# State update ahead of the state read, and the first chunk reordered with M first, long lines and whole weight pieces

## The chip, the cores and the metric

The kernel runs on one core of one Trainium2 chip. Times are device microseconds (us) of one execution. Before: median 628.86 us of the four runs taken beside the changed kernel (626.38 to 630.35). The granted clock of TensorE is given where it matters.

PE is TensorE, PEld its weight load, DVE is VectorE, ACT is ScalarE, POOL is GpSimd, SP is SyncE; SPq and ACTq are the queues in which SP and ACT issue transfers. L311 is line 311 of the kernel concerned.

## The reference

An mLSTM cell (4 batches, 8 heads, 768 steps, head size 40) is followed by a two-layer block with exact GELU (320 to 2048 to 320). The weights of the block come as 64-bit floats.

```python
for t in range(S):
    m_new = np.maximum(f_gate[:, :, t] + m, i_gate[:, :, t])
    C = exp(f + m - m_new) * C + exp(i - m_new) * (v outer k)     # n likewise, with k
    y[:, :, t] = sigmoid(o_gate) * (C q) / max(|n q|, 1)
...
x = attn_out.transpose(0, 2, 1, 3).reshape(B * S, H * D)
h = x @ w_in
g = 0.5 * h * (1.0 + erf(h / sqrt(2)))
return g @ w_out
```

## The kernel before

The 768 steps are cut into 6 chunks of 128. For each chunk and batch the cell computes scores (k times q), multiplies them with weights W made from the running maximum M, reads the state with q, updates the state with k and v, and turns the result y into xT. "Up" (xT times w_in, then GELU) and "down" (g times w_out) follow for all four batches at once. Down matmuls of one chunk fill the gaps of the cell of the next. During the first chunk, the weights are loaded as raw 64-bit words and converted to 32-bit floats in 26 pieces: 10 of w_in, 16 of w_out.

The parts that matter here, cut:

```python
# weight pieces: two transfers of 64 partitions each, lines of 1 KB
src = w_src["in"][blk * R:(blk + 1) * R, 2 * f0:2 * (f0 + 2 * WP)]
src = src.rearrange("k (m two x) -> k m two x", two=2, x=2 * P)
pieces.append(([(slice(R * e, R * e + R), src[:, :, e, :]) for e in range(2)], w_in[...]))
...
def fetch(i):
    bits[i] = raw.tile([P, WP, 2], U32, name="bits", tag="bits", bufs=NB)[...]
    for r, src in parts:
        nc.sync.dma_start(out=bits[i][r]..., in_=src)

def scores(self, b):
    ...                                          # ps: k times q; then W = ps * W on DVE
    pf = ps_h.tile([P, H + NP, D1], F32, name="pf", tag="h")
    pc = pf[:, H:H + NP, :]                      # read and update share one bank
    if c > 0:
        ...nc.tensor.matmul(pf[r, ...], qT[:, p, r], state[b][:, p, :])       # read
        nc.vector.tensor_tensor(out=self.far[b], in0=pf[:, 0:H, :], in1=gT)   # far
    if c + 1 < NCH:
        ...nc.tensor.matmul(pc[...], kb[n % NLD][...], vw[...])               # update
        ...                                      # state = state * dec + pc (POOL, DVE)

def values(self, b):                             # ph = W times v; hs = ph (+ far); y from hs

for n in range(B):                               # SP, at the start
    if n > 0:
        load(n)                                  # q, k, v, output gate of one batch
    fetch(n)
```

## Time and profile before

| | before |
|---|---|
| median of 4 runs | 628.86 us |
| span of the profiled execution | 627.3 us, granted clock 0.961 |
| first up matmul | 70.14 us |
| cell of chunk 1 resumes on PE | 127.90 us |
| up of chunks 1 to 5 starts at | 184.19, 278.68, 373.16, 467.63, 554.50 us |
| PE waits ahead of the update, chunks 1 to 4 | 19.5 us in 16 waits |
| DVE waits for pieces of w_in | 9.3 us in 4 waits |

The start times divide the kernel in two: up to about 128 us the converting of weights and the first cell set the pace, and after that every chunk takes 94.5 us with PE nearly full. Two lines of before that the prediction doesn't show are wanted later. The first is from the page's 40 slices (15.7 us each): the mean busy share of the core's 16 DMA engines, in tenths.

```profile
DMA  9999199735430034530034530035200010000000
```

In the first seven slices (110 us) the transfer engines are full, except in slice 5. The second is from DVE's waits (line waited for: us in total, times, longest):

```profile
DVE pow L219 <- DMA bits<-in_moe_w_in_dram: 9.3, 4, 3.3
```

`pow` is the first operation of a piece's conversion, `bits` the raw piece. The conversions seldom wait for their data.

### The profile page before, as it was taken

What the parts mean: (1) busy time and instruction counts of PE and PEld (TensorE: products, weight loads), DVE (VectorE), ACT (ScalarE), POOL (GpSimd) and SP (SyncE); (2) the same over time, 40 slices, a digit from 0 to 9 for tenths busy, and PEclk for the clock granted to TensorE, in tenths of its full rate; (3) what the DMA queues carried; (4) which work ended last, traced back from release to release, by engine and by line L of the source; (5) the groups of instructions that cost most, each with busy time, mean ns of one, the idle gap of its engine ahead of it and who ended that gap; (6) DMA issues with size and microseconds to landing.
All of it is one profiled execution on the core that took longest, in us unless ns stands there. A gap on an engine that the chain in (4) does not pass through costs nothing.

```text
span 627.3 us, 9450 instructions
## 1 busy us (share of the span) xinstructions
PE 554.4 (88%) x3850; PEld 358.1 (57%) x3850; DVE 199.0 (32%) x442; ACT 230.1 (37%) x516; POOL 81.3 (13%) x130
## 2 busy tenths in 40 slices
PE   0637698778999998899999899999899999999997
PEld 0536354456764466764476664476664477754575
DVE  5457686834630013630013630013630014500000
ACT  0775274683022283022284022284022293122200
POOL 4212300012230011230011230011220001100000
PEclk9967699889999999999999999999999999999999
DMA  9999199735430034530034530035200010000000
GB/s 161 208 211 184 37 161 207 178 104 103 76 64 0 1 112 90 82 64 2 0 108 92 81 67 1 0 101 96 46 22 0 1 44 13 11 11 0 1 21 21
DMA packets 136233, 43.62 MB, mean 70 GB/s; under 512 B 101248, under 2 KB 134048, under 8 KB 136192
## 3 DMA queue, kind: packets, MB, share of 16 engines
q1 hardware_dynamic: 132976, 41.36, 33.3%
q10 hardware_dynamic: 3216, 1.67, 1.0%
q8 instruction: 30, 0.49, 0.4%
q14 instruction: 11, 0.09, 0.1%
HBM read 38.99 MB, written 4.03 MB: 69 GB/s over the span
## 4 chain that ended last, share of the span: by engine, by line
PE 49%; issue 38%; POOL 6%; DMA 3%; SPq 2%; DVE 1%; POOLq 0%; ACTq 0%; ACT 0%; DVEq 0%
PE po L403 25%; PE pu L388 11%; PE ph L329 3%; PE ps L293 3%; POOL state L320 2%; POOL Mb L254 2%; DMA Mb<-M_d 2%; PE pf L303 2%; PE pf L311 2%; PE pt L276 2%; SPq L102 2%; PE px L355 1%; SPq L208 1%; POOL vw L286 1%; DMA M_d<-M 1%
## 5 line engine op out<-in xcount | busy, mean ns | idle before, releaser
L403 PE MATMUL po<-w_out,g 128*128 128x320 f32 x768 | 221.0, 437 | 0.0
L388 PE MATMUL pu<-xT,w_in 64*128 64x512 f32 x960 | 215.5, 604 | 3.2 <-ACT g L391 2.8
L403 PEld LDWEIGHTS po<-w_out,g 128*128 128x128 f32 x768 | 141.2, 191 | 52.6 <-issue 1.2
L388 PEld LDWEIGHTS pu<-xT,w_in 64*128 64x128 f32 x960 | 100.6, 192 | 115.7 <-issue 109.5
L296 DVE TENSOR_TENSOR W<-ps,W 128x512 f32<-128x512 f32 x48 | 30.9, 685 | 259.0 <-PE ps L293 259.0
L391 ACT ACTIVATE g<-pu 128x512 f32<-128x512 f32 x96 | 52.0, 593 | 131.9 <-PE pu L388 131.9
L357 ACT COPY xT<-px 64x384 f32<-64x384 f32 (+1 forms) x48 | 17.9, 420 | 128.3 <-DVE xT L356 128.3
L257 ACT ACTIVATE W<-Mb,aT 128x128 f32<-128x128 f32 x192 | 58.1, 393 | 1.8 <-POOL Mb L254 1.7
L320 POOL TENSOR_TENSOR state<-state,dec 64x164 f32<-64x164 f32 x32 | 14.8, 462 | 286.2 <-PE pf L303 285.0
L311 PE MATMUL pf<-vw,kb 128*64 128x41 f32 x320 | 14.1, 239 | 32.1 <-POOL state L320 19.5
L254 POOL TENSOR_SCALAR_AFFINE_SELECT Mb<-Mb 128x1024 f32<-128x1024 f32 x24 | 27.0, 1145 | 80.2 <-DMA Mb<-M_d 80.0
L406 ACT COPY o_sb<-po 128x320 f32<-128x320 f32 x24 | 10.2, 426 | 61.5 <-PE po L403 40.7
L311 PEld LDWEIGHTS pf<-vw,kb 128*64 128x64 f32 x320 | 12.2, 146 | 35.0 <-POOL state L320 21.7
L338 POOL TENSOR_TENSOR y<-hs,ob 128x320 f32<-128x320 f32 x24 | 19.4, 809 | 97.8 <-DVE hs L332 72.1
L293 PEld LDWEIGHTS ps<-qT,kT 64*128 64x128 f32 x384 | 25.8, 205 | 10.1 <-issue 10.1
L293 PE MATMUL ps<-qT,kT 64*128 64x128 f32 x384 | 30.4, 302 | 0.0
L329 PE MATMUL ph<-vb,W 128*64 128x41 f32 x768 | 28.6, 236 | 0.0
L329 PEld LDWEIGHTS ph<-vb,W 128*64 128x64 f32 x768 | 26.4, 145 | 2.4 <-issue 2.2
L356 DVE COPY xT<-px 64x384 f32<-64x384 f32 (+1 forms) x48 | 21.1, 476 | 17.5 <-PE px L355 16.7
L276 PE MATMUL pt<-ident,kb 128*128 128x128 f32 x96 | 17.2, 308 | 9.3 <-ACT kT L279 9.3
L279 ACT COPY kT<-pt 128x512 f32<-128x512 f32 x24 | 14.0, 584 | 30.8 <-PE pt L276 30.6
L355 PE MATMUL px<-ident,y 128*128 128x128 f32 x120 | 18.4, 287 | 6.8 <-ACT xT L357 6.0
(71 smaller groups left out, 352.9 us busy)
## 6 DMA issues: line engine op xcount, KB each, us to landing
Mb<-M_d SPq DMA_DIRECT2D x21, 512.0 KB, 4.0
bits<-in_moe_w_in_dram SPq DMA_DIRECT2D x20, 256.0 KB, 5.6
bits<-in_moe_w_out_dram SPq DMA_DIRECT2D x16, 320.0 KB, 4.2
qb<-in_q_dram SPq DMA_DIRECT2D x24, 160.0 KB, 4.4
kb<-in_k_dram SPq DMA_DIRECT2D x24, 160.0 KB, 4.8
vb<-in_v_dram SPq DMA_DIRECT2D x24, 160.0 KB, 4.3
ob<-in_o_gate_dram SPq DMA_DIRECT2D x24, 160.0 KB, 3.9
out_dram<-o_sb SPq DMA_DIRECT2D x24, 160.0 KB, 1.8
```

What stands on the lines that cost most here:

```text
L254: nc.gpsimd.affine_select(out=M_n, in_=M_n, compare_op=OP.is_ge, fill=1.0e30, base=0, pattern=[[0, H], [1, L]], channel_multiplier=-1)
L257: nc.scalar.activation(out=W[n][:, h, :], in_=M_n[:, h, :], func=AF.Exp, scale=-1.0, bias=aT[:, c, b * H + h:b * H + h + 1])
L276: nc.tensor.transpose(pt[:, p, :], src[n % NLD][:, 2 * p:2 * p + 2, :].rearrange("p h d -> p (h d)"), ident)
L293: nc.tensor.matmul(ps[hip][:, p, :], kT[r, p, :], qT[r, p, :], start=True, stop=True)
L296: nc.vector.tensor_tensor(out=w, in0=ps[hip], in1=w, op=OP.mult)
L311: nc.tensor.matmul(pc[halves[hip], p, :], kb[n % NLD][:, 2 * p + hip, :], vw[:, 2 * p + hip, :], start=True, stop=True)
L320: nc.gpsimd.tensor_tensor(out=st, in0=st, in1=d.to_broadcast([DP, NP, D1]), op=OP.mult)
L329: nc.tensor.matmul(ph[r, h, :], Pm[:, h, r], vb[n % NLD][:, h, :], start=True, stop=True)
L355: nc.tensor.transpose(px[:, k, :], ys[:, (k0 + k) * R:(k0 + k + 2) * R], ident)
L388: nc.tensor.matmul(pu[e], w_in[r, k, f // 2 * P:(f // 2 + 1) * P], xT[r, (k - e) % NK, :], start=(k == 0), stop=(k == NK - 1))
L391: nc.scalar.activation(out=g[:, f + e, :], in_=pu[e], func=AF.Gelu)
L403: nc.tensor.matmul(po, g[:, f, b * L:(b + 1) * L], w_out[:, f, :], start=(f == 0), stop=(f == NF - 1))
```

## The change

There are two intents. In the cell, the update goes ahead of the read in their common bank, so that PE doesn't wait for DVE's `far` between the two. In the first chunk, M of the chunk is computed alone and sent first, into four buffers instead of three and in long lines; the work of the batches is put in the order in which tiles should arrive; and each weight piece becomes one transfer with lines of 4 KB.

The diff, cut to its core:

```diff
@@ weight pieces
-            src = src.rearrange("k (m two x) -> k m two x", two=2, x=2 * P)
-            pieces.append(([(slice(R * e, R * e + R), src[:, :, e, :]) for e in range(2)],
-                           w_in[:, blk, f0 // 2:f0 // 2 + WP]))
+            pieces.append((src.rearrange("k (two x) -> two k x", two=2), w_in[:, blk, f0 // 2:f0 // 2 + WP]))
...
-        for r, src in parts:
-            to = bits[i][r].rearrange("p n two -> p (n two)")
-            if len(src.shape) == 3:
-                to = to.rearrange("p (m x) -> p m x", x=2 * P)
-            nc.sync.dma_start(out=to, in_=src)
+        nc.sync.dma_start(out=bits[i].rearrange("p n two -> p (n two)"), in_=src)
@@ M first
-    NM = 3
+    NM = 4
-    M_d = dram.tile([BH, S], F32, name="M_d")
+    M_d = dram.tile([NCH, BH, L], F32, name="M_d")
+    for c0, c1 in ((0, 1), (1, NCH)):            # scans of chunk 0 alone, then of the rest
...
+        if c0 == 0:
+            nc.scalar.dma_start(out=M_d[0], in_=M[:, 0])
+            for n in range(B):
                 load_M(n, nc.scalar)
@@ scores
             pc = pf[:, H:H + NP, :]
+            if c + 1 < NCH:
+                (the 8 update matmuls)
             if c > 0:
                 (the 8 read matmuls, far)
             if c + 1 < NCH:
-                (the 8 update matmuls)
                 (scaling and adding of the state)
@@ first chunk
+        def run_first(self):
+            self.turn(0), weights_of(0), convert(0)
+            decays()
+            self.scores(0), weights_of(1), convert(1)
+            self.turn(1), weights_of(2), weights_of(3), output_gate(0), self.values(0), convert(2)
+            self.scores(1), self.turn_y(0), output_gate(1), self.values(1), convert(3)
+            self.turn(2), self.scores(2), self.turn_y(1), output_gate(2), self.values(2), convert(4)
+            self.turn(3), self.scores(3), self.turn_y(2), output_gate(3), self.values(3), convert(5)
+            self.turn_y(3)
```

`turn` transposes k and q of a batch (kT, qT), `weights_of` makes W from M, `turn_y` transposes y into xT, `convert` handles one weight piece, and `decays` prepares the decay factors of the state. The up steps are renumbered for the columns that a piece now holds; their number and sizes stay.

More of the change, by code (lines that the diff above doesn't have):

```diff
@@ L53 @@
     NLD = 6
-    NM = 3
+    NM = 4
     NB = 4
     WP = 512
-    assert S % L == 0 and DFF % (4 * WP) == 0 and DM % R == 0 and DM <= WP and D <= DP and NLD > B == 4
+    assert S % L == 0 and DFF % (4 * WP) == 0 and DM % R == 0 and DM <= WP and D <= DP and NLD > B == NM == 4
     const = ctx.enter_context(tc.tile_pool(name="const", bufs=1))
@@ L112, in load_M @@
         Mb[n] = wts.tile([P, H, L], F32, name="Mb", tag="Mb", bufs=NM)
-        eng.dma_start(out=Mb[n], in_=M_d[b * H:(b + 1) * H, c * L:(c + 1) * L]
-                      .unsqueeze(0).to_broadcast([P, H, L]))
+        eng.dma_start(out=Mb[n].rearrange("p h l -> p (h l)"),
+                      in_=M_d[c, b * H:(b + 1) * H, :].rearrange("h l -> (h l)").unsqueeze(0).to_broadcast([P, H * L]))
     nc.sync.dma_start(out=f_sb.rearrange("p c l -> p (c l)"), in_=f_gate.rearrange("b h s -> (b h) s"))
@@ L146 @@
     nc.vector.memset(m0[:, 0:1], -1.0e30)
-    nc.vector.tensor_tensor_scan(out=bl.rearrange("p c l -> p (c l)"), data0=keep.rearrange("p c l -> p (c l)"),
-                                 data1=f_sb.rearrange("p c l -> p (c l)"), initial=0.0, op0=OP.mult, op1=OP.add)
-    nc.vector.tensor_tensor(out=a, in0=i_sb, in1=bl, op=OP.subtract)
-    for c in range(NCH):
-        nc.vector.tensor_tensor_scan(out=M[:, c], data0=a[:, c], data1=a[:, c], initial=m0[:, c:c + 1],
-                                     op0=OP.max, op1=OP.max)
-        if c == 0:
-            nc.scalar.dma_start(out=M_d[:, 0:L], in_=M[:, 0])
-            for n in range(NM):
+    for c0, c1 in ((0, 1), (1, NCH)):
+        flat = lambda t: t[:, c0:c1].rearrange("p c l -> p (c l)")
+        nc.vector.tensor_tensor_scan(out=flat(bl), data0=flat(keep), data1=flat(f_sb), initial=0.0,
+                                     op0=OP.mult, op1=OP.add)
+        nc.vector.tensor_tensor(out=a[:, c0:c1], in0=i_sb[:, c0:c1], in1=bl[:, c0:c1], op=OP.subtract)
+        for c in range(c0, c1):
+            nc.vector.tensor_tensor_scan(out=M[:, c], data0=a[:, c], data1=a[:, c], initial=m0[:, c:c + 1],
+                                         op0=OP.max, op1=OP.max)
+            if c + 1 < NCH:
+                nc.vector.tensor_tensor(out=m0[:, c + 1:c + 2], in0=bl[:, c, L - 1:L], in1=M[:, c, L - 1:L],
+                                        op=OP.add)
+        if c0 == 0:
+            nc.scalar.dma_start(out=M_d[0], in_=M[:, 0])
+            for n in range(B):
                 load_M(n, nc.scalar)
-        if c + 1 < NCH:
-            nc.vector.tensor_tensor(out=m0[:, c + 1:c + 2], in0=bl[:, c, L - 1:L], in1=M[:, c, L - 1:L], op=OP.add)
-    nc.scalar.dma_start(out=M_d[:, L:S], in_=M[:, 1:NCH].rearrange("p c l -> p (c l)"))
     nc.vector.tensor_tensor(out=ew, in0=a[:, 0:NCH - 1],
@@ L165, with gates_turned, decays @@
                             in1=M[:, 1:NCH], op=OP.subtract)
+    def gates_turned(parts):
+        for src, dst in parts:
+            n = dst.shape[1]
+            pg = ps_tr.tile([P, n, BH], F32, name="pg", tag="tr")
+            for c in range(n):
+                nc.tensor.transpose(pg[:, c, :], src[:, c, :], ident[0:BH, 0:BH])
+            nc.vector.tensor_copy(out=dst, in_=pg)
+    gates_turned([(a, aT)])
     nc.scalar.activation(out=ew, in_=ew, func=AF.Exp)
     nc.scalar.activation(out=gg, in_=gg, func=AF.Exp)
-    for src, dst in ((a, aT), (ew, ewT), (gg, gT)):
-        n = dst.shape[1]
-        pg = ps_tr.tile([P, n, BH], F32, name="pg", tag="tr")
-        for c in range(n):
-            nc.tensor.transpose(pg[:, c, :], src[:, c, :], ident[0:BH, 0:BH])
-        nc.vector.tensor_copy(out=dst, in_=pg)
-    pd = ps_tr.tile([P, NCH - 1, BH], F32, name="pd", tag="tr")
-    nc.tensor.matmul(pd.rearrange("p c n -> p (c n)"), last, gT.rearrange("p c n -> p (c n)"), start=True, stop=True)
-    nc.vector.tensor_copy(out=dec, in_=pd)
-    gate_ctx.close()
-    gp = ctx.enter_context(tc.tile_pool(name="gp", bufs=1))
+    def decays():
+        gates_turned([(ew, ewT), (gg, gT)])
+        pd = ps_tr.tile([P, NCH - 1, BH], F32, name="pd", tag="tr")
+        nc.tensor.matmul(pd.rearrange("p c n -> p (c n)"), last, gT.rearrange("p c n -> p (c n)"),
+                         start=True, stop=True)
+        nc.vector.tensor_copy(out=dec, in_=pd)
     w_src = {}
@@ L190 @@
             src = w_src["in"][blk * R:(blk + 1) * R, 2 * f0:2 * (f0 + 2 * WP)]
-            src = src.rearrange("k (m two x) -> k m two x", two=2, x=2 * P)
-            pieces.append(([(slice(R * e, R * e + R), src[:, :, e, :]) for e in range(2)],
-                           w_in[:, blk, f0 // 2:f0 // 2 + WP]))
+            pieces.append((src.rearrange("k (two x) -> two k x", two=2), w_in[:, blk, f0 // 2:f0 // 2 + WP]))
     n_in = len(pieces)
     for f in range(NF):
-        pieces.append(([(slice(0, P), w_src["out"][f * P:(f + 1) * P, :])], w_out[:, f, :]))
+        pieces.append((w_src["out"][f * P:(f + 1) * P, :], w_out[:, f, :]))
     bits, sig, pow2 = {}, {}, {}
@@ L201, in fetch @@
             return
-        parts, dst = pieces[i]
+        src, dst = pieces[i]
         bits[i] = raw.tile([P, WP, 2], U32, name="bits", tag="bits", bufs=NB)[:, 0:dst.shape[1], :]
-        for r, src in parts:
-            to = bits[i][r].rearrange("p n two -> p (n two)")
-            if len(src.shape) == 3:
-                to = to.rearrange("p (m x) -> p m x", x=2 * P)
-            nc.sync.dma_start(out=to, in_=src)
+        nc.sync.dma_start(out=bits[i].rearrange("p n two -> p (n two)"), in_=src)
     def convert(i):
@@ L235, in convert @@
             fetch(i + NB)
-    for n in range(B):
-        if n > 0:
-            load(n)
-        fetch(n)
+    fetch(0)
+    load(1)
+    fetch(1)
+    load(2)
+    fetch(2)
+    load(3)
+    fetch(3)
+    nc.sync.dma_start(out=M_d[1:NCH].rearrange("c p l -> p c l"), in_=M[:, 1:NCH])
     halves = (slice(0, R), slice(R, P))
@@ L299, in scores @@
             pc = pf[:, H:H + NP, :]
+            if c + 1 < NCH:
+                for p in range(NP):
+                    for hip in range(2):
+                        nc.tensor.matmul(pc[halves[hip], p, :], kb[n % NLD][:, 2 * p + hip, :], vw[:, 2 * p + hip, :],
+                                         start=True, stop=True)
             if c > 0:
@@ L308, in scores @@
             if c + 1 < NCH:
-                for p in range(NP):
-                    for hip in range(2):
-                        nc.tensor.matmul(pc[halves[hip], p, :], kb[n % NLD][:, 2 * p + hip, :], vw[:, 2 * p + hip, :],
-                                         start=True, stop=True)
                 for hip in range(2):
@@ L380, in up_steps, with step @@
     def up_steps(g):
-        def step(f):
+        def step(i):
+            f = i // (WP // P) * 2 * (WP // P) + i % (WP // P)
             pu = [ps_mm.tile([P, TG], F32, name="pu", tag="mm") for e in range(2)]
-            for k in range(NK):
+            for blk in range(NK):
                 for e in range(2):
                     r = halves[e]
-                    nc.tensor.matmul(pu[e], w_in[r, k, f // 2 * P:(f // 2 + 1) * P], xT[r, (k - e) % NK, :],
-                                     start=(k == 0), stop=(k == NK - 1))
+                    nc.tensor.matmul(pu[e], w_in[r, blk, i * P:(i + 1) * P], xT[r, (blk - e) % NK, :],
+                                     start=(blk == 0), stop=(blk == NK - 1))
             for e in range(2):
-                nc.scalar.activation(out=g[:, f + e, :], in_=pu[e], func=AF.Gelu)
-        return [lambda f=f: step(f) for f in range(0, NF, 2)]
+                nc.scalar.activation(out=g[:, f + e * (WP // P), :], in_=pu[e], func=AF.Gelu)
+        return [lambda i=i: step(i) for i in range(NF // 2)]
     def down_steps(c, g):
@@ L417, in feeder @@
         return fill
-    conv = feeder([lambda i=i: convert(i) for i in range(len(pieces) + 1)])
-    first = feeder([lambda: conv(1)] * (n_in // 2 + 1))
-    Cell(0).run(first)
+    Cell(0).run_first()
+    gate_ctx.close()
+    gp = ctx.enter_context(tc.tile_pool(name="gp", bufs=1))
+    conv = feeder([lambda i=i: convert(i) for i in range(n_in // 2 + 1, len(pieces) + 1)])
     for c in range(NCH):
```

## The prediction

> **What bounds the kernel now.** I read the page first: busy shares, then the 40 slices.
>
> ```profile
> span 627.3 us, 9450 instructions
> PE 554.4 (88%) x3850; PEld 358.1 (57%) x3850; DVE 199.0 (32%) x442; ACT 230.1 (37%) x516; POOL 81.3 (13%) x130
> ...
> PE   0637698778999998899999899999899999999997
> ```
>
> PE is busy for 88% of the span, and the holes sit in two places: slices 1 to 8 (the first chunk, with the weights being converted) and one thin slice per chunk after it. So the two halves of the change hit two different regimes, and I size each by its own stage. The table of stretches (cut at round numbers near the first and last up matmuls of the timeline; busy us with counts for PE, PEld, DVE, ACT, POOL, then granted clock, DMA share, GB/s) says the same:
>
> ```profile
> 45.00:70.00 25.00, 16.02 (x206) 13.74 (x202) 19.15 (x41) 11.91 (x27) 8.76 (x10) 0.70 0.74 136
> 70.00:105.00 35.00, 34.57 (x140) 17.71 (x140) 24.94 (x56) 20.29 (x35) 0.00 (x0) 0.91 0.85 157
> 128.00:184.00 56.00, 51.12 (x476) 38.93 (x476) 24.43 (x54) 21.27 (x56) 14.21 (x20) 0.97 0.47 94
> 184.00:219.00 35.00, 35.00 (x163) 15.68 (x163) 0.00 (x0) 9.48 (x17) 0.00 (x0) 1.00 0.02 5
> ```
>
> From 128 us on, PE has no company in being full: 51.1 of 56 us in a cell stretch, 35 of 35 in an up stretch, granted clock 0.97 to 1.00. The 4.9 us that are missing in the cell stretch are one gap, four times. The timeline of one batch shows it:
>
> ```profile
> 141.69 1.16 PE L293 MATMUL ps<-qT,kT 64*128 64x128 f32 x16
> 142.78 0.79 PE L303 MATMUL pf<-state,qT 128*64 128x82 f32 x16
> 142.95 1.29 DVE L296 TENSOR_TENSOR W<-ps,W 128x512 f32<-128x512 f32 x2 [5.79 <-PE ps L293]
> 143.66 1.00 POOL L320 TENSOR_TENSOR state<-state,dec 64x164 f32<-64x164 f32 x2 [5.80 <-PE pf L303]
> 144.16 0.49 DVE L306 TENSOR_TENSOR far<-pf,gT 128x328 f32<-128x328 f32 x1
> 144.79 0.67 PE L311 MATMUL pf<-vw,kb 128*64 128x41 f32 x16 [1.22 <-POOL state L320]
> 145.25 1.14 PE L329 MATMUL ph<-vb,W 128*64 128x41 f32 x32
> ```
>
> The label "POOL state" is misleading. In program order the scaling of the state comes after these matmuls, so they cannot depend on it. L311 waits on DVE and on POOL; its POOL input (vw) is long done. DVE's far (L306), which reads the other part of the same pf tile, ends at 144.65, and PE goes 0.14 later; L320 merely ends at the same moment. The view of waits has the sum: PE pf L311 <- POOL state, 19.5 us in 16 waits.
>
> In the first chunk the chain of waits goes through the fourth M tile:
>
> ```profile
> 34.18 0.53 SPq L113 DMA_DIRECT2D Mb<-M_d  x1
> 41.24 1.09 POOL L254 TENSOR_SCALAR_AFFINE_SELECT Mb<-Mb 128x1024 f32<-128x1024 f32 x1 [19.63 <-DMA Mb<-M_d]
> 42.30 0.74 POOL L286 TENSOR_TENSOR vw<-vb,ewT 128x328 f32<-128x328 f32 x1
> 43.10 1.08 PE L311 MATMUL pf<-vw,kb 128*64 128x41 f32 x16 [10.53 <-POOL vw L286]
> ```
>
> With three buffers the fourth M waits for a buffer and for its turn on SP, lands at 41.1, holds POOL, POOL holds vw, and PE stands for 10.5 us. The first up matmul starts at 70.14.
>
> **What the Trainium skill says.** "PSUM — Partial Sum Buffer", section "PSUM bank collisions raise a hardware error": PE and VectorE must not touch one bank and quadrant together, even at other columns, so the wait is guarded by bank. The trace agrees: L311 writes other columns than far reads, and still starts only after far. The order, not the wait, has to change. "DMA: Bandwidth & Descriptors", "Rules for kernel authors", advises one 128-partition transfer instead of two to disjoint halves, which is what the weight pieces become. The trace of before has only the halves (median landing 5.8 us under load); it cannot yet say. "TensorE: Matmul & The Clock Gate", Part 1, gives half clock after an idle window and full clock after about 3.4 us of sustained work. The trace has a mean granted clock of 0.63 at 43 to 56 us and 0.60 at 70 to 78, and the up matmuls stay slow for about 6 us, longer than the page says.
>
> **Part 1: update ahead of read, chunks 1 to 4.** Nothing is added or removed: 8 update and 8 read matmuls per batch exchange places. The update needs vw, which POOL finished well before (147.86 + 0.74 = 148.60 for the batch whose scores start at 153.85), and the bank, which was free for the read anyway. The read then follows with no reader in between, and values (L329) use another bank. So each of 4 x 4 batches loses the 1.22 us gap: 16 x 1.22 = 19.5 us. A check: a cell stretch of chunk 4 from its end of up to the next up is about 59.9 us (94.5 us period less 34.6); that of the last chunk, which has no update, is 554.57 - 502.24 = 52.3. The difference 7.6 is 4 x (1.22 + 0.67), gap plus update, exactly. Does a new wait replace it? DVE now gets far 0.67 us later, at scores + 2.55 instead of + 2.47, because its two products W (1.29 us) end only there; the POOL scaling ends at about + 3.5, DVE's addition at about + 4.3, hs at about + 4.8, against 146.43 + 0.50 - 141.69 = + 5.2 before. y is needed two down parts later. The last turn of y in a chunk (y ready at 178.25, used at 181.40) has 3 us of slack. I find nothing, so all 19.5 us count, since PE is full up to the end.
>
> **Part 2: the first chunk.** What arrives sooner: the scan over chunk 0 alone takes 0.5 us in place of 1.75, the subtraction 0.25 in place of 0.94, so M_d is issued at about 4.4 instead of 6.3, and lands near 9. Four M loads follow by 12; at 512 KB and the 300 GB/s of the stretch after 13 us they take 1.4 to 1.7 us each, so the last is there by 17 to 20 instead of 41. The 10.5 us wait at 43 goes. But the new order is serial: turn(b) stands behind values(b-1) and a conversion. By hand, with the durations of before: ACT free at 12; table 1.28, two exponentials 1.45, kT and qT 1.1, W of batch 0 2.45: 17.8; conversion (two of 0.72) and state 2.0; W 2.45, conversion 1.45, kT and qT 1.1, two W 4.9, table 1.28, sigmoid 0.39, hs 0.43: hs of batch 0 ends near 32 (before: 49.99). Batch 1 to hs: den and y on DVE 2.1, five conversion operations 2.95, W 1.29, values 1.5, copy 0.5: 8.3, so 40.5. Batches 2 and 3 each go den 2.1, first conversion operation 0.45, two on ACT 1.45, kT and qT 1.1, scores 1.7, update 0.75, turn of y 1.3, values 1.5, hs 0.5: 10.9 with PE at its low clock, 9.5 with the full one. That gives hs of batch 3 at 62 (59.5), where before it was 64.3. Tail: den 2.1, conversion 3, copy of xT 0.5 to 0.9: up begins at 68 (65.5) instead of 70.14. The 18 us head start is nearly eaten by 11 us per batch, where before took 5.9, 4.7 and 3.7. Gain: 2 to 5 us, I take 2.5.
>
> **After it**, up and conversion of chunk 0 run from 70.14 to the end of PE's wait at 127.9 (6.97 us for ACT kT). That stretch is paced by 20 conversions (DVE 2.1 us each for the output weights, DMA share 0.85), which neither moves nor shrinks, so it shifts as a whole. The input pieces as one transfer save issue time on SP (one of 0.6 us instead of two), but not on this path.
>
> Sum: 629.06 - 19.5 - 2.5 = 607.1.
>
> **The rivals.** First: the first chunk gains in full, 10 us or more, because the 10.5 us wait goes and the batches overlap better than I add up (a warm PE, arrivals earlier). For it: the hole is large and its cause removed. Against: the engine order puts kT of the next batch behind the conversion's ACT work, which waits for DVE's den. It would give about 598 to 600. Second: the first chunk gets slower, since this serial order costs more than the earlier M gives, for instance if long M lines starve the tile loads (160-byte lines, about 1.3 us per tensor): up starts at 73 and the time is 612. Third: the update takes over the wait, because vw comes late or because the reader of the bank is still there; part 1 then gives half, 617. The slack of 5 us on vw speaks against it. A fourth, that the denser PE is throttled: up stretches with PE 35 of 35 ran at 1.00, so no.
>
> **Range and chances.** Part 1 is safe to about 1.5 us; part 2 is a hand sum of some 30 terms in which each batch can be off by 1.5 us, so -3 to +8. Together 600 to 613. Two per cent is 616.5; only the third rival gets there. Faster 0.95, same 0.045, slower 0.005.
>
> **What would show it.** Right: no PE wait before the update in chunks 1 to 4, the read directly after it, a chunk period of about 89.6 us instead of 94.5; M tiles landed by 20 us; hs of batch 0 near 32, then about 10 us per batch, up at 66 to 68; the stretch from there to chunk 1 again 58 us. Wrong: a new wait of PE on vw or on DVE in the cells, hs steps below 8 us (then below 602), or a first up matmul after 71.

## The result, and the profile after

The changed kernel is **slower**: median 661.98 us of four runs (660.97 to 662.31) against 628.86. The ratio is 1.0528 (95% interval 1.0492 to 1.0564). Ratios here are the mean time of one kernel's runs over that of the other's of the same rounds, so not quite the ratio of the medians quoted. The predicted 607.1 and its whole range are missed, in the wrong direction.

| | before | after |
|---|---|---|
| first up matmul | 70.14 | 100.99 |
| cell of chunk 1 resumes on PE | 127.90 | 183.56 |
| between the two | 57.8 | 82.6 |
| up of chunk 1 | 184.19 | 234.36 |
| up of chunk 5 | 554.50 | 587.44 |
| period of a chunk (chunks 2 to 4) | 94.5 | 88.7 |

So 55.7 us are lost by the time that the cell of chunk 1 resumes (30.9 ahead of the first up, 24.8 in the stretch after it). Then 22.7 are won: 5.5 until up of chunk 1, three times 5.7 to up of chunk 4, and nothing in the last chunk, which has no update. 55.7 - 22.7 = 33.0, which is the difference of the starts of the last up, 587.44 - 554.50 = 32.9.

**The cells do what was meant.** One batch in the timeline of the changed kernel (start, us, engine, line, operation, output from inputs, count):

```profile
196.18 1.16 PE L299 MATMUL ps<-qT,kT 64*128 64x128 f32 x16
197.27 0.67 PE L309 MATMUL pf<-vw,kb 128*64 128x41 f32 x16
...
197.75 0.77 PE L314 MATMUL pf<-state,qT 128*64 128x82 f32 x16
198.36 1.08 PE L336 MATMUL ph<-vb,W 128*64 128x41 f32 x32
198.64 0.49 DVE L317 TENSOR_TENSOR far<-pf,gT 128x328 f32<-128x328 f32 x1
```

No line of PE has a wait behind it, and `far` runs beside the values. From the scores' start to the values' start it is 2.18 us, where before it was 3.56 (141.69 to 145.25 in the prediction's fence).

**The first third is starved of data, while the transfer engines stand idle.** The page's slices after:

```profile
PE   1323348527789999999999999999999999999997
...
DMA  7433411359637500155300554002500000000000
```

PE is at 1 to 4 tenths for 100 us (slices of 16.5 us). The row of the DMA engines, which was at 9, is now at 7, 4, 3, 3, 4, 1, 1 in the same time. DVE's waits name the data that is missing:

```profile
DVE pow L221 <- DMA bits<-in_moe_w_in_dram: 63.0, 9, 11.8
```

63.0 us in 9 waits in place of 9.3 in 4. The timeline has the moments at which pieces come (in brackets: idle time before, and what ended it):

```profile
106.88 0.43 DVE L221 TENSOR_SCALAR pow<-bits 128x512 uint32<-128x512 uint32 x1 [5.61 <-DMA bits<-in_moe_w_in_dram]
...
117.04 0.43 DVE L221 TENSOR_SCALAR pow<-bits 128x512 uint32<-128x512 uint32 x1 [7.34 <-DMA bits<-in_moe_w_in_dram]
...
127.25 0.43 DVE L221 TENSOR_SCALAR pow<-bits 128x512 uint32<-128x512 uint32 x1 [7.40 <-DMA bits<-in_moe_w_in_dram]
```

One piece every 10.2 us: 524,288 bytes in 10.2 us are 51.4 GB/s. Two short stretches in which only a piece is under way show how many engines carry it (stretch, busy us and counts of the five engines, granted clock, DMA share, GB/s):

```profile
103.50:106.50 3.00, 3.00 (x12) 1.50 (x10) 0.00 (x0) 0.00 (x0) 0.00 (x0) 0.70 0.13 53
...
120.50:122.50 2.00, 2.00 (x7) 1.60 (x5) 0.00 (x0) 0.00 (x0) 0.00 (x0) 0.50 0.13 53
```

A DMA share of 0.13 is 2 of 16 engines. And 2 is the outermost size of the piece's source, `two k x`.

**Other transfers suffer too.** The start of the changed kernel:

```profile
4.38 0.97 SPq L210 DMA_DIRECT2D bits<-in_moe_w_in_dram  x1
...
6.41 13.18 SPq L102 DMA_DIRECT2D kb<-in_k_dram  x1
...
7.92 15.75 ACTq L113 DMA_DIRECT2D Mb<-M_d  x4
...
23.35 0.43 DVE L221 TENSOR_SCALAR pow<-bits 128x512 uint32<-128x512 uint32 x1 [11.77 <-DMA bits<-in_moe_w_in_dram]
...
23.70 1.28 ACT L178 ACT_TABLE_LOAD   x1 [23.70 <-DMA bits<-in_moe_w_in_dram]
```

The first piece is issued at 4.38 and is there at 23.35. SP's issue of k of the next batch, two transfers later, takes 13.18 us, and the issue of the four M by ACT 15.75. SP is free at 19.59 and ACT at 23.67, 0.3 us after DVE takes up the piece, and ACT can't begin its first table load and exponentials until 23.70, where before it began at 16.15.

### The profile page after: what moved, and what is told of

It reads as the page before. It is cut to its first block, busy times and chain, and to the rows that moved or that the text cites. A ratio compares the mean times of both kernels' runs of the same rounds, so it can differ in the third digit from the quotient of the medians.

```text
span 660.3 us, 9428 instructions
## 1 busy us (share of the span) xinstructions
PE 559.4 (85%) x3850; PEld 365.5 (55%) x3850; DVE 199.7 (30%) x444; ACT 230.6 (35%) x516; POOL 80.0 (12%) x130
## 4 chain that ended last, share of the span: by engine, by line
PE 72%; DMA 13%; SPq 8%; DVE 5%; ACT 1%; issue 1%; DVEq 0%; ACTq 0%
PE po L422 32%; PE pu L407 26%; DMA bits<-in_moe_w_in_dram 9%; SPq L102 7%; PE ps L299 4%; PE ph L336 3%; PE pt L282 3%; DMA bits<-in_moe_w_out_dram 2%; DMA M_d<-M 2%; PE pf L314 2%; PE px L362 2%; PE pf L309 2%; DVE sig L228 1%; DVE pow L221 1%; DVE pow L233 1%
## 5 line engine op out<-in xcount | busy, mean ns | idle before, releaser
L407 PE MATMUL pu<-xT,w_in 64*128 64x512 f32 x960 | 221.3, 615 | 26.4 <-ACT g L410 22.8
L407 PEld LDWEIGHTS pu<-xT,w_in 64*128 64x128 f32 x960 | 108.3, 195 | 137.0 <-issue 104.8
L302 DVE TENSOR_TENSOR W<-ps,W 128x512 f32<-128x512 f32 x48 | 30.9, 686 | 258.6 <-PE ps L299 258.6
L223 ACT ACTIVATE pow<-pow,e_hi 128x320 f32<-128x320 uint32 (+1 forms) x26 | 16.2, 623 | 73.2 <-DVE pow L221 73.2
L221 DVE TENSOR_SCALAR pow<-bits 128x320 uint32<-128x320 uint32 (+1 forms) x26 | 10.3, 397 | 69.9 <-DMA bits<-in_moe_w_in_dram 63.0
L425 ACT COPY o_sb<-po 128x320 f32<-128x320 f32 x24 | 10.2, 426 | 54.9 <-PE po L422 39.7
L362 PE MATMUL px<-ident,y 128*128 128x128 f32 x120 | 19.5, 299 | 3.2 <-DVE y L351 3.2
```

The source lines that it names most:

```text
L302: nc.vector.tensor_tensor(out=w, in0=ps[hip], in1=w, op=OP.mult)
L362: nc.tensor.transpose(px[:, k, :], ys[:, (k0 + k) * R:(k0 + k + 2) * R], ident)
L407: nc.tensor.matmul(pu[e], w_in[r, blk, i * P:(i + 1) * P], xT[r, (blk - e) % NK, :], start=(blk == 0), stop=(blk == NK - 1))
```

## The experiments

There are two theories. **A:** the loss is the whole piece's transfer alone: its outermost dimension of 2 keeps it on 2 of 16 engines, where it is slow itself and holds up what comes after. **B:** the loss is the new order of the first chunk (serial, or M's long lines starving the tiles), the prediction's second rival. A third question is what the update order, M first and the order are each worth without the pieces.

### First four: the parts alone

**e1**: the kernel before, with the update ahead of the read and nothing else.

```diff
             pc = pf[:, H:H + NP, :]
+            if c + 1 < NCH:
+                (the 8 update matmuls)
             if c > 0:
                 (read, far)
             if c + 1 < NCH:
-                (the 8 update matmuls)
```

> The kernel before with the state update put ahead of the state read, nothing else. Theory A (the loss of the whole change is all in the first chunk, from the weight pieces that run on 2 of 16 DMA engines): the update order itself saves what the chunk period of the changed kernel shows, 94.5 - 88.7 = 5.8 us in each of 4 chunks, so 629 - 23 = 606 us. Rival B (the new order of the first chunk is the loss): also 606. Rival C (the update order gains less in the old kernel, 1.22 us x 16 alone): 609.5.

Measured: 605.35 us, ratio 0.9616 (0.9592 to 0.9641), 23.9 less than the 629.2 of before in these rounds. First up is at 70.92, so the first chunk is as before, and the 16 waits of 19.5 us are gone from PE's list.

**e2**: the changed kernel, but each piece again as two transfers of 64 partitions, with the new 4 KB lines.

```diff
-            pieces.append((src.rearrange("k (two x) -> two k x", two=2), w_in[...]))
+            src = src.rearrange("k (two x) -> two k x", two=2)
+            pieces.append(([(slice(R * e, R * e + R), src[e]) for e in range(2)], w_in[...]))
...
-        nc.sync.dma_start(out=bits[i].rearrange("p n two -> p (n two)"), in_=src)
+        for r, src in parts:
+            nc.sync.dma_start(out=bits[i][r].rearrange("p n two -> p (n two)"), in_=src)
```

> The changed kernel with each input weight piece loaded by two transfers of 64 partitions, the same 4 KB lines, so that the source's outermost dimension is 64 and not 2. Theory A: a piece lands in 3 to 8 us in place of 10 to 18, the first up matmul starts near 68 us, and the time falls by 50 us or more, to 600 to 608 us. Rival B (serial order of the first chunk): the time stays above 640. Rival D (4 KB lines at a row pitch of 16 KB are slow in themselves): also above 640, and pieces still land late.

Measured: 606.94 us, ratio 0.9645 (0.9621 to 0.9669). The same bytes into the same places with the same line length, and the loss is gone. First up is at 72.27, and from there to the cell of chunk 1 it is 56.6 us. The same three issues as above, in the timeline of e2:

```profile
4.66 1.64 SPq L212 DMA_DIRECT2D bits<-in_moe_w_in_dram  x2
...
7.92 0.37 SPq L102 DMA_DIRECT2D kb<-in_k_dram  x1
...
7.99 2.17 ACTq L113 DMA_DIRECT2D Mb<-M_d  x4
```

k takes 0.37 us instead of 13.18, the four M 2.17 instead of 15.75. So the standing of both queues comes from the form of the pieces. By what means a slow transfer holds a queue's issuing, the trace doesn't show.

**e3**: the kernel before, with whole pieces (and the up steps renumbered for them) and nothing else.

```diff
-            src = src.rearrange("k (m two x) -> k m two x", two=2, x=2 * P)
-            pieces.append(([(slice(R * e, R * e + R), src[:, :, e, :]) for e in range(2)], ...))
+            pieces.append((src.rearrange("k (two x) -> two k x", two=2), ...))
```

> The kernel before with whole weight pieces alone (and the column order that goes with them). Theory A: 10 pieces at 10 us each or more on two engines, and every other transfer behind them on those two: 45 to 60 us slower than before, 670 to 690 us. Rival B: as before, 629. Rival D: slower as well.

Measured: 683.83 us, ratio 1.0869 (1.0845 to 1.0893); first up at 111.54. With e1 and e2 this makes a square, and the whole pieces cost the same on both sides of it:

| | pieces in halves | whole pieces | difference |
|---|---|---|---|
| kernel before | 629.2 | 683.83 (e3) | +54.6 |
| changed kernel | 606.94 (e2) | 661.98 | +55.0 |

Theory A holds, and B falls: the loss comes with the pieces in either order, and it is 55 us, not 33. The rest of the change makes up for 22 of it. (661.98 is from an earlier group of rounds, in which before had 628.86.)

**e4**: the kernel before, with M first (four buffers, long lines, scans of chunk 0 ahead) and its old order of the first chunk.

```diff
-    NM = 3
+    NM = 4
...
+    for c0, c1 in ((0, 1), (1, NCH)):
...
+            nc.scalar.dma_start(out=M_d[0], in_=M[:, 0])
+            for n in range(B):
                 load_M(n, nc.scalar)
```

> The kernel before with M first and in long lines, four M buffers, the rest of M written later from SP; old weights, old order of the first chunk, old update order. Theory A: the fourth M tile lands by 20 us instead of 41, PE's wait of 10.5 us goes, the old overlapping order keeps its 4 to 6 us per batch, and the first up matmul starts 6 to 12 us sooner: 617 to 623 us. Rival (tile loads set the pace instead of M): 626 to 629.

Measured: 626.14 us, ratio 0.9955 (0.9936 to 0.9973); first up at 67.86. The gain of 3 us is under 2%, but clear of the noise (the interval leaves out 1); I had expected the first up 6 to 12 us sooner, and it came 2.3. The timeline says where the rest went:

```profile
32.73 2.23 PE L343 MATMUL ph<-vb,W 128*64 128x41 f32 x32 [3.99 <-DVE W L310]
...
44.02 0.43 DVE L229 TENSOR_SCALAR pow<-bits 128x512 uint32<-128x512 uint32 x1 [5.05 <-DMA bits<-in_moe_w_in_dram]
44.36 0.42 DVE L234 TENSOR_SCALAR sig<-bits 128x512 uint32<-128x512 uint32 x1
44.48 0.72 ACT L231 ACTIVATE pow<-pow,e_hi 128x512 f32<-128x512 uint32 x1
...
46.47 0.43 ACT L348 COPY hs<-ph 128x328 f32<-128x328 f32 x1
```

PE has made the values of batch 0 by 35.0, but ACT copies them to `hs` only at 46.47 (end 46.90, before 49.99). In the old order, conversions and the four output gates stand ahead of that copy on ACT, and the last of these conversions waits until 44.02 for its piece to arrive. So M first alone moves the hole from PE to ACT.

### Four sizes of the outermost dimension

If A is right, the number of engines must follow the outermost size and the time must follow with it. These four kernels load pieces of the same 512 KB, 128 partitions and 4 KB lines in one transfer, from 128 rows of w_in instead of 64. They differ only in a, the size of the outermost dimension of the source. They load wrong weights, and so give wrong results; the work is the same.

```diff
-            src = w_src["in"][blk * R:(blk + 1) * R, 2 * f0:2 * (f0 + 2 * WP)]
-            pieces.append((src.rearrange("k (two x) -> two k x", two=2), w_in[...]))
+            r0 = min(blk * R, DM - P)
+            src = w_src["in"][r0:r0 + P, 2 * f0:2 * (f0 + WP)]
+            pieces.append((src.rearrange("(k a) x -> a k x", a=4), w_in[...]))     # a = 2, 4, 8, 16
```

> Control for the next three; the result is wrong on purpose (other rows of the weights are read). The changed kernel, each input piece still one transfer of 128 lines of 4 KB, but rows are taken as 2 groups of 64 instead of the two halves: outermost dimension 2. Theory A (the number of DMA engines is set by the outermost dimension): as the changed kernel, 662 us, and a DMA share of 2/16 = 0.125 where only a piece is in flight. Rival D (the halves' addresses or the line length): could differ.

> Wrong on purpose. The same transfer, rows as 4 groups of 32: outermost dimension 4. Theory A: 4 engines, DMA share 0.25 where only a piece is in flight, a piece takes 5.1 us in place of 10.2; the time falls to 615 to 630 us. Rival D (line length, one transfer of 128 lines): 662 as before.

> Wrong on purpose. Outermost dimension 8. Theory A: 8 engines, share 0.5, about 2.6 us per piece; 606 to 612 us. Rival D: 662.

> Wrong on purpose. Outermost dimension 16. Theory A: all engines, about 1.5 us per piece when alone; the time of the version with two half pieces, 607 us within 3 us. Rival D: 662.

Measured, with 629.96 us for before and two runs of each:

| a | us | ratio | first up |
|---|---|---|---|
| 2 | 662.65 | 1.0521 | 101.38 |
| 4 | 626.00 | 0.9939 | 84.89 |
| 8 | 612.26 | 0.9721 | 75.05 |
| 16 | 606.33 | 0.9627 | 72.03 |

DVE's waits for pieces, a = 2, 4, 8 and 16 in turn (four kernels, the same line of each):

```profile
DVE pow L222 <- DMA bits<-in_moe_w_in_dram: 61.9, 9, 11.4
```

```profile
DVE pow L222 <- DMA bits<-in_moe_w_in_dram: 21.5, 4, 7.4
```

```profile
DVE pow L222 <- DMA bits<-in_moe_w_in_dram: 5.6, 3, 3.9
```

For a = 16 the line reads 2.4 us in 1 wait. With a = 2 the kernel takes what the changed kernel took, with other addresses and other rows; with a = 16 it takes what e2 took, in one transfer. It is not the one transfer that is slow, then, nor the 4 KB lines, but the outermost size. The number of engines itself shows where nothing but pieces is under way (columns as above), first for a = 4 and then for a = 8:

```profile
67.50:73.00 5.50, 2.26 (x22) 2.03 (x22) 2.89 (x6) 2.40 (x4) 0.00 (x0) 0.63 0.26 104
```

```profile
59.75:62.25 2.50, 0.85 (x8) 0.85 (x10) 1.49 (x3) 1.60 (x3) 0.00 (x0) 0.50 0.50 131
```

Shares of 0.26 and 0.50 are 4 and 8 of 16 engines. Twice the engines give twice the rate from 2 to 4 (53 and 104 GB/s), but not from 4 to 8 (131); why, no run shows. The time with a = 8 was expected at 606 to 612 us and lies just above; the other three came as expected.

### What the order of the first chunk is worth

**e5** is e4 with the update order as well, so it is the change with the old pieces and the old first-chunk order.

```diff
 (e4, and the update ahead of the read as in e1)
```

> Before with M first in long lines and four M buffers, and the state update ahead of the read; old first-chunk order, old weight pieces. If the two gains add: 629.2 - 3.1 - 23.9 = 602.2 us, faster than the changed kernel with half pieces (606.9). If the new first-chunk order were worth something, it would have to be slower than 606.9.

**e6** is the changed kernel with the pieces of before in full (halves, 1 KB lines, old columns), so it differs from e5 in the order of the first chunk alone.

```diff
-            pieces.append((src.rearrange("k (two x) -> two k x", two=2), ...))
+            src = src.rearrange("k (m two x) -> k m two x", two=2, x=2 * P)
+            pieces.append(([(slice(R * e, R * e + R), src[:, :, e, :]) for e in range(2)], ...))
```

> The changed kernel with the old weight pieces (two transfers of 64 partitions in 1 KB lines) and their column order; everything else as changed. It tells the line length from the number of engines. Theory A: as with half pieces in 4 KB lines, 606.9 within 1%. Rival (lines of 4 KB are worth something on all engines): 610 or more. Against the run with M first, the update order and the old first-chunk order it shows the first-chunk order alone: expected 4 to 5 us slower, since its first up matmul started at 72.3 us against 67.9.

Measured beside 628.26 us for before: e5 602.59, ratio 0.9585 (0.9552 to 0.9618), first up at 67.98; e6 604.77, ratio 0.9628 (0.9596 to 0.9661), first up at 70.39. The new order brings nothing; the traces have it 2.4 us later at the first up, and the times lean the same way (2.2 us, where 4 to 5 were expected), but their intervals overlap. Long lines of the pieces brought nothing either: e2 with 4 KB lines 0.9645, e6 with 1 KB lines 0.9628.

e6 is also the clean test of my hand sum for the first chunk. Its copies of `hs` and its first up:

```profile
31.93 0.41 ACT L347 COPY hs<-ph 128x328 f32<-128x328 f32 x1
...
40.25 0.43 ACT L347 COPY hs<-ph 128x328 f32<-128x328 f32 x1
...
51.50 0.43 ACT L347 COPY hs<-ph 128x328 f32<-128x328 f32 x1
...
62.56 0.43 ACT L347 COPY hs<-ph 128x328 f32<-128x328 f32 x1
...
70.39 33.17 PE L412 MATMUL pu<-xT,w_in 64*128 64x512 f32 x140 [3.60 <-DVE xT L369]
```

The ends are 32.3, 40.7, 51.9 and 63.0. The steps of 8.3, 11.3 and 11.1 are long because each batch's turn and scores stand behind the conversion of the batch before.

### An order that overlaps

The head start of batch 0 (32 against 50 us) is lost to these serial steps. **e7** is e6 with the turn of the next batch, and for batch 1 its scores too, put ahead of the values of the current one.

```diff
             decays()
-            self.scores(0), weights_of(1), convert(1)
-            self.turn(1), weights_of(2), weights_of(3), output_gate(0), self.values(0), convert(2)
-            self.scores(1), self.turn_y(0), output_gate(1), self.values(1), convert(3)
-            self.turn(2), self.scores(2), self.turn_y(1), output_gate(2), self.values(2), convert(4)
-            self.turn(3), self.scores(3), self.turn_y(2), output_gate(3), self.values(3), convert(5)
+            self.scores(0), self.turn(1), weights_of(1), convert(1)
+            weights_of(2), weights_of(3), self.scores(1), output_gate(0), self.values(0)
+            self.turn(2), convert(2), output_gate(1), self.values(1), self.turn_y(0)
+            self.scores(2), self.turn(3), convert(3), output_gate(2), self.values(2), self.turn_y(1)
+            self.scores(3), convert(4), output_gate(3), self.values(3), self.turn_y(2)
+            convert(5)
             self.turn_y(3)
```

> As the changed kernel with the old weight pieces (604.8 us), but in the first chunk the turn of a batch stands before the values of the one before it, and its scores before the conversion that waits for DVE. Theory (the new order of the first chunk costs 11 us per batch because the copy of kT stands on ACT behind a conversion that waits for the den chain on DVE): hs of batch 0 stays near 32 us, the steps to the next fall from 11 to about 8 us, the first up matmul starts at 60 to 63 us instead of 70.4, and the time falls to 595 to 598 us. Rival (the first chunk is held by the arrival of tiles or of weights, or PE at low clock): steps stay at 10 to 11 us, time within 3 us of 604.8.

**e8** is e7 with the last conversion behind the last turn of y.

```diff
-            convert(5)
-            self.turn_y(3)
+            self.turn_y(3), convert(5)
```

> The same, with the sixth conversion behind the last turn of y. If the conversion's five DVE operations before the last copy of xT delay the first up matmul, it starts another 3 us sooner; but the conversions that follow in the up stage set when chunk 1 can begin, so the time should fall by 0 to 3 us against the run above.

Measured beside 628.1 us for before: e7 595.14, ratio 0.9476 (0.9457 to 0.9495), first up at 60.29; e8 **594.09**, ratio 0.9460 (0.9443 to 0.9478). In e8:

```profile
36.97 0.41 ACT L347 COPY hs<-ph 128x328 f32<-128x328 f32 x1
...
52.09 0.43 ACT L347 COPY hs<-ph 128x328 f32<-128x328 f32 x1
...
58.35 29.50 PE L412 MATMUL pu<-xT,w_in 64*128 64x512 f32 x120 [0.22 <-DVE xT L369]
```

These are batches 1 and 3 and the first up, 3.3, 10.5 and 12.0 us ahead of e6. Up of chunk 1 starts at 166.06 instead of 175.89, and the time is 10.7 less than e6's. Both are right in their results, and e8 is the fastest of all kernels here. That e8 beats e7 is not settled: their intervals overlap.

## Why the prediction was wrong

**The step that failed** is in the last lines of "After it": "The input pieces as one transfer save issue time on SP (one of 0.6 us instead of two), but not on this path." I sized the issue of the transfer and never the transfer. Each piece went from two transfers to one that runs on 2 of 16 engines: one piece every 10.2 us, for ten pieces that the conversions of the first chunk and of the stretch after it wait for. Its cost is 55 us in both halves of the square above. With it, the prediction's own sum would have been 607.1 + 55 = 662, which is what was measured (its two other errors nearly cancel, as shown below).

**Why I missed it.** I cited "DMA: Bandwidth & Descriptors", "Rules for kernel authors", for its advice on one 128-partition transfer in place of two halves, and stopped there. Another row of the same table, "Use all 16 engines", says that an outermost dimension of size c below 16 confines the whole transfer to at most c engines. The Trainium skill's "DMA: Bandwidth & Descriptors", section "Why a DMA increments its semaphore by 16 and not by 1", gives the count: the largest number up to 16 that divides the slowest dimension other than 1 of both access patterns. Here that is 2 of `two k x` against 128 partitions. The traces agree (DMA share 0.13, 0.26 and 0.50 with outermost sizes 2, 4 and 8), and so do the times of the kernels with a = 2 to 16. The diff had the whole evidence: the rearrangement is made so that one transfer can write both halves, and it is what puts 2 outermost.

**No rival was of this kind.** I had M's long lines as a possible starver and a slow serial order (612), and an update that waits anew (617). None was slower than before, and "slower" had a chance of 0.005. A transfer that changes form needs a rival of its own.

**The update order was right in kind and too small in size.** Predicted: 16 x 1.22 = 19.5 us. Measured: the period falls by 5.7 us in place of 4.9, and e1 gains 23.9 in all. Per batch, scores to values falls by 3.56 - 2.18 = 1.38. Of this 1.22 is the gap. The rest, about 0.16, is that the read used to run out in full before PE stood still (0.79), and now the next burst starts 0.61 after it (197.75 to 198.36). My check of 7.6 us with the last chunk should have shown this and agreed partly by luck: it added the update at its full 0.67 us, but what follows starts 0.46 us after the update does (144.79 to 145.25). In the last chunk of before it is 1.72 us from scores to values (517.72 to 519.44), so a batch differs by 3.56 - 1.72 = 1.84, not by the 1.89 of the check, and the 0.16 was inside. (The check's 554.57 and 502.24 are 554.50 and 502.17 in the trace; the difference is the same.)

**M first was right**, under its condition: in e2 the four M are issued by 10.2 us and the last is selected on POOL at 19.4, against the "by 17 to 20" that I gave for landing. In the changed kernel itself ACT stood at these issues until 23.67; the first select is at 16.24 and the other three run from 28.75 to 31.9, right behind POOL's `vw`, whose chain of waits goes back to the exponentials and the copy of kT that ACT began only then.

**The serial order was right**: `hs` at 32, 40.5, 51.4 and 62 predicted, 32.3, 40.7, 51.9 and 63.0 in e6; up at 68 predicted, 70.39 measured, 1.0 of it from the last `hs` and the rest from the tail behind it (7.4 us where I had 6). So part 2 without the pieces gains nothing, and not the 2.5 I took. The stretch of 58 us behind it held in e2 (56.6); with the slow pieces it became 82.6.

**The sum.** Of the terms, -19.5 was about -23, -2.5 was about 0 (e6 against e1: 0.9628 and 0.9616, intervals overlapping), and 0 for the pieces was +55.

What stays open: what exactly holds the queues' issuing while a slow transfer is under way, how the 55 us divide into the pieces' own slowness and the delay of others, and whether the new order of the first chunk costs 2 us or nothing.

## What to carry to other kernels

When two transfers are merged into one, write down the outermost size of both access patterns: a rearrangement that makes the merge possible may put a 2 outermost, and here the merged transfer then ran on two engines at about 26 GB/s each and stalled its neighbours. A DMA share that sits at a small multiple of 1/16 while engines wait for data is the sign to look for. Size every transfer that a diff touches by its bytes and its engines, not by its issue alone, and after a head start has been won, look whether the order of the engines spends it again: 10 us lay there.

## What the Trainium skill lacked or had wrong

- "DMA: Bandwidth & Descriptors", "Rules for kernel authors", the row on two transfers to disjoint partition halves says not to bother and to use one transfer. As the change followed it, that took the kernel from 606.94 us (halves, e2) to 661.98. Here the advice was harmless only with 16 outermost in the merged transfer (a = 16: 606.33), and it brought nothing then; the row should point to the row "Use all 16 engines".
- The same table states the limit of c engines but not what it does to others. Here the next transfers, of other tensors and with 128 outermost, were held as well: SP stood 13.18 us at one issue of k (0.37 in e2), ACT 15.75 us at four of M (2.17 in e2).
- "DMA: Bandwidth & Descriptors", "Specifications", has about 27 GiB/s per engine (29 GB/s). Pieces alone with 4 KB lines made 53 GB/s on two engines and 104 on four, about 26 per engine, some 10% less; on eight engines it was 131, about 16 per engine.
- "TensorE: Matmul & The Clock Gate", Part 1, has full clock after about 3.4 us of sustained work, with the moment varying by 500 ns either way. In the clock record kept with the traces, the up matmuls that start at 70.14 us in before get full clock at 76.45, and those that start at 100.99 and 119.51 in the changed kernel at 105.30 and 125.78: after 6.3, 4.3 and 6.3 us. In the changed kernel the clock had fallen at 118.95, inside one idle time of PE that ended at 119.51. It is 2.87 us long by PE's modelled ends and 3.69 by the weight loads, so the traces don't say whether it was shorter than the page's idle window of about 3.4 us, and no run varied it.
